# First experts of a fused attention and mixture kernel: weight splits and conversions in other slots, one more product by seven

## The chip, the cores and the metric

One Trainium2 chip, one of its cores. The metric is the device time of one execution in microseconds (us), the median over the runs. PE is TensorE, DVE VectorE, ACT ScalarE, POOL GpSimd, SP the engine that issues nearly all transfers.

## What is computed

```python
kv  = einsum('bhsd,bhse->bhde', k, v)
out = einsum('bhsd,bhde->bhse', q, kv)
x   = out / rms(out) * g_norm              # 2304 tokens x 512
h   = x @ w_in                             # 512 x 2048
x   = (h * sigmoid(h)) @ w_out             # back to 512
p   = domain_probs / sum(domain_probs)     # 4 experts
out = sum_e p[:, e] * (relu(x @ w1[e]) @ w2[e])   # 512 x 1024 each
```

## The kernel before, in words

Tokens stand in three thirds of 768 columns; `acc` in SBUF holds all of them, 512 rows deep. The hidden width is cut into groups of 512: four for the first mixture (the "first experts", groups 0 to 3) and eight for the second. A **step** is one group with one third of the tokens. Steps -12 to -1 are the first experts', 0 to 23 the second's; steps -9 to -7 are group 1, -6 to -4 group 2, -3 to -1 group 3.

A step has a **first product** (tokens by `w1`) and a **second product** (hidden values by `w2`, added to `acc`). The second product of step n runs interleaved with the first product of step n + 1. Every operand is split into a high and a low half: ACT writes the high half (`hi`, L149), DVE or POOL the low half (`lo`, L152), and three matmuls stand for one.

Both products multiply 2 x 2 blocks. "By seven" (`seven_events`, L626) does it with seven block products and sums of blocks (Winograd's form of Strassen); "by blocks" (`plain_events`, L651) with eight. `seven(n)` (L138) says which second products are by seven. Each block product is 12 matmuls of 128x128 by 128x384. For seven, the weights need sums s1 to s4 besides a11, a12, a22 (`SUMS`, L216), the hidden values c11 to c22 need sums t1 to t4 (`sumh`, L451), and the results in PSUM are read after every block product: for the first product by `keep` (ACT, L407) and `add` (DVE, L412), for the second by `gather` (DVE, L457). There is one bank `ps_ox` and one `ps_oz`; a gather must have read its bank before the next block product into it begins, two block products of the second product (four of PE's) after the one it reads. The seven run in the order b11, t1, t2, b22, t3, b21, t4 (`ORDER`, L80), the gathers as `GATHER` (L81) lists them.

The weights of the first experts come as 64-bit integers' words that the kernel turns into floats: `load_wd` (SP), `cv1` and `cv2` (ACT), `cv3` and `cv4` (DVE: L196, L197, L201), `cv5` (POOL, L207). There are two stage buffers, so a load waits for the `cv5` of two conversions before. A group has eight **conversions** of 128x512, four for `w1` and four for `w2`. Then sums (`fsum`, L230) and splits (`fhi`, `flo`, L253 and L258) make the weights of the products; three of a group's seven first weights (numbers 1, 4 and 6) get their low half on POOL.

Nothing schedules at run time. Each event is put at a **slot**, a number; slots count PE's block products, `start[n]` is the first slot of step n, and `after` is the start of the next one. `events` (L707) sorts all events by slot, and each engine takes its own in that order. So a table of slots (`SUM_AT`, `SPLIT_AT`, `CONVERT`, and the numbers in L580 to L587) is the order of every queue. The second experts' weights have tables of their own: `W1_AT` and `W2_AT` (L673 and L677).

```python
put(after + 2 * m, self.again, n, k)          # second product, block m
put(after + 2 * m + 1.1, self.gather, ...)    # L647; 0.25 for m = 6 of the first experts
```

Of the kernel before, what the change touches and what calls it, by code (L numbers as in the profile page):

```python
# [65 lines left out]
class Net:  # L66
# [70 lines left out]

    def seven(self, n):  # L138

        return n >= 1 or n in (-9, -8, -7, -5, -4, -3)  # L140

    def pair(self, n):
        return (n + F1) % NP
# [66 lines left out]
    def quarter(self, e, i, name):  # L210
# [6 lines left out]
        s1=("a21", "a22", ALU.add), s2=("s1", "a11", ALU.subtract), s3=("a11", "a21", ALU.subtract),  # L217
        s4=("a12", "s2", ALU.subtract),
    )

    SUM_AT = {1: (5, 5.1, 6.5, 8), 2: (15.4, 15.5, 16.8, 18), 3: (7.6, 7.7, 12, 14)}
    SPLIT_AT = {
        1: dict(a11=6, s4=7.2, s3=8.6, s1=10.8, s2=11.8, a12=14.8, a22=16),
        2: dict(a11=2.4, a12=4.4, a21=6.4, a22=14.5, s1=15.9, s4=17.1, s3=18.3, s2=29.2),
        3: dict(a11=6, s1=8.5, s2=10.5, s4=12.5, s3=14.5, a12=16, a22=18, a21=18.2),
    }

    CONVERT = {1: (6.5, 9, 18.5, 20.5, 22.5, 25.5, 31, 35), 2: (6, 8.5, 15, 19.2, 20.8, 22.4, 24, 31.8)}
# [317 lines left out]
    def first_events(self, put):  # L546

        pool = self.nc.gpsimd
        for n in range(-F1, 0):
            e, t = self.group(n), self.pair(n)  # L550
            b0, after = self.start[n], self.start[n + 1]
            if e == 0 and t == 2:
                for b, (i, j) in enumerate(self.PLAIN):
                    at, name = b0 + 4 * b, f"c{i + 1}{j + 1}"
# [22 lines left out]
                (self.seven_events if self.seven(n) else self.plain_events)(put, n)  # L577
            if t == 0:
                if e > 0:
                    for name, at in (("s1", -6.6), ("s2", -6.5), ("s3", -1.6), ("s4", -1.5)):  # L580
                        put(b0 + at, self.fsum, e, 0, name)
                    for k in range(7):
                        put(b0 - 9 + 2 * k, self.fhi, e, 0, k)
                        put(b0 - 8.6 + 2 * k, self.flo, e, 0, k, pool if k in (1, 4, 6) else None)
                        if self.A[k][0] == "s":
                            put(b0 + (-1.4 if k == 2 else -8.5 + 2 * k), self.done_sum, e, 0, self.A[k])
                    put(b0 + 3.6, self.done_full, e, 0)  # L587
                    for at, name in zip(self.SUM_AT[e], ("s1", "s2", "s4", "s3")):
                        put(b0 + at, self.fsum, e, 1, name)
                    for name, at in self.SPLIT_AT[e].items():  # L590
                        put(b0 + at, self.fhi, e, 1, name)
                        put(b0 + at + 0.4, self.flo, e, 1, name)
                        if name[0] == "s":
                            put(b0 + max(at + 0.5, self.SUM_AT[e][2] + 0.1 if name in ("s1", "s2") else 0), self.done_sum, e, 1, name)
                    put(b0 + max(*self.SUM_AT[e], *(at for name, at in self.SPLIT_AT[e].items() if name[0] == "a")) + 0.5, self.done_full, e, 1)
                if e + 1 < E1:
                    for i in range(2):
                        for c in range(4):
                            k = 4 * i + c
                            if e == 0 and k < 3:  # L600
                                continue
                            at = b0 + self.CONVERT[e][k] if e else after + 9 + 2.4 * k
                            a = 4 * (e + 1) + c, i
                            if (e, k) != (0, 3):
                                put(max(at - 5.7, b0 + self.CONVERT[e][k - 2] + 1.5) if e and k > 1 else at - 5.7, self.load_wd, *a)
                            put(at, self.cv1, *a)
                            put(at + 0.01, self.cv2, *a)
                            put(at + 0.5, self.cv3, *a)
                            put(at + 0.8, self.cv4, *a)
                            put(at + 1.2, self.cv5, *a)  # L610
            if e == 0 and t == 2:
                for k, name in enumerate(("t1", "t2", "t3", "t4")):
                    at = b0 + 0.5 + 3 * k
# [376 lines left out]
```

## Time and profile before

| what | value |
|---|---|
| median of 3 runs | 1147.36 us (1146.85 to 1147.37) |
| the profiled execution's own time | 1146.34 us |
| its span, first to last instruction | 1144.6 us |
| mean granted TensorE clock | 0.999 |
| PE busy | 1134.5 us (99%), 6673 matmuls |
| DVE busy | 950.2 us (83%) |
| ACT busy | 515.7 us (45%) |
| POOL busy | 335.1 us (29%) |

A row of the timeline gives an instruction's start, its duration, engine, line, what it writes and reads, and in brackets how long its engine had been idle and who released it. A row with x12 is one block product. Matmuls are pipelined, so a product's row is a little longer than the distance to the next. An instruction's duration on DVE and POOL includes time in which it was held up after it had been issued.

### The profile page before, as it was taken

The page shows a single profiled execution, that of the slowest core. Times are in us where ns is not written, and L with a number is a line of the kernel's source. Part 1 is how long each engine was busy: PE and PEld are TensorE (multiplying, and loading weights), DVE is VectorE, ACT ScalarE, POOL GpSimd, SP SyncE. Part 2 cuts the span into 40 slices and gives each one's busy share as a digit, 9 for nine tenths or more (in the row PEclk, how much of TensorE's full clock was granted, in tenths as well). Part 3 has the DMA queues.
Part 4 walks back from the last instruction along what each step waited for, and adds up shares of the span by engine and source line. Part 5 has one row for each costly group of instructions (what it writes and reads, how often), then busy time and mean ns, then how long its engine had stood idle before and what let it go on. Part 6 is the DMA issues. An engine that isn't in the chain of part 4 may idle for free.

```text
span 1144.6 us, 17104 instructions
## 1 busy us (share of the span) xinstructions
PE 1134.5 (99%) x6673; PEld 1128.5 (99%) x6673; DVE 950.2 (83%) x1080; ACT 515.7 (45%) x730; POOL 335.1 (29%) x198
## 2 busy tenths in 40 slices
PE   9999999999999999999999999999999999999998
PEld 8999999999999999999999999999999999999998
DVE  3997768987987587699799899899889889889874
ACT  4885565555554454544333333333333333333334
POOL 4943213331221344132232222232232232223211
PEclk9999999999999999999999999999999999999999
DMA  9967876666656662695675776675686685686604
GB/s 365 361 241 259 296 294 245 219 208 222 229 191 212 196 235 100 249 311 196 237 240 205 234 253 203 217 253 202 216 268 208 204 271 198 205 278 207 207 32 162
DMA packets 70035, 261.23 MB, mean 228 GB/s; under 512 B 7804, under 2 KB 26180, under 8 KB 69444
## 3 DMA queue, kind: packets, MB, share of 16 engines
q1 hardware_dynamic: 69668, 260.11, 65.2%
q8 instruction: 53, 0.87, 0.3%
q14 instruction: 26, 0.21, 0.1%
q10 hardware_dynamic: 288, 0.04, 0.0%
HBM read 222.34 MB, written 37.79 MB: 227 GB/s over the span
## 4 chain that ended last, share of the span: by engine, by line
PE 88%; DVE 6%; DMA 2%; ACT 2%; issue 1%; POOL 0%; SPq 0%; DVEq 0%; ACTq 0%; POOLq 0%
PE ps_x L369 22%; PE ps_ox L369 19%; PE ps_z L369 16%; PE ps_oz L369 15%; PE ps_o L498 9%; PE ps_h L397 4%; DMA kv_raw<-in_kv 2%; DVE hid L152 1%; ACT hid L149 1%; PE p_o L858 1%; PE ps_kv L836 1%; DVE acc L467 1%; DVE f L454 1%; DVE f L414 1%; ACT f L424 1%; DMA wd_raw<-in_wd 1%
## 5 line engine op out<-in xcount | busy, mean ns | idle before, releaser
L149 ACT ACTIVATE hid<-f 128x768 fp32r<-128x768 f32 x231 | 192.1, 843 | 370.4 <-DVE f L454 195.4
L152 POOL TENSOR_TENSOR hid<-f,hid 128x768 fp32r<-128x768 f32 x82 | 162.9, 1987 | 569.9 <-ACT hid L149 438.4
L369 PE MATMUL ps_x<-x,w 128*128 128x384 f32 x1584 | 297.0, 335 | 0.0
L369 PEld LDWEIGHTS ps_x<-x,w 128*128 128x128 f32 x1584 | 277.7, 188 | 0.0
L369 PE MATMUL ps_ox<-hid,w 128*128 128x384 f32 x1392 | 261.4, 335 | 0.6 <-DVE acc L467 0.6
L369 PEld LDWEIGHTS ps_ox<-hid,w 128*128 128x128 f32 x1392 | 243.2, 188 | 1.0 <-ACT hid L149 0.9
L369 PE MATMUL ps_z<-x,w 128*128 128x384 f32 x1188 | 222.8, 335 | 0.0
L369 PEld LDWEIGHTS ps_z<-x,w 128*128 128x128 f32 x1188 | 208.3, 188 | 0.0
L369 PE MATMUL ps_oz<-hid,w 128*128 128x384 f32 x1044 | 196.4, 335 | 1.8 <-DVE acc L467 1.3
L152 DVE TENSOR_TENSOR hid<-f,hid 128x768 fp32r<-128x768 f32 x149 | 153.0, 1028 | 52.3 <-ACT hid L149 52.2
L369 PEld LDWEIGHTS ps_oz<-hid,w 128*128 128x128 f32 x1044 | 182.3, 188 | 3.0 <-DVE acc L467 2.0
L498 PE MATMUL ps_o<-hid,w 128*128 128x384 f32 x672 | 124.2, 334 | 0.0
L454 DVE TENSOR_TENSOR f<-f 128x768 f32<-128x768 f32 x116 | 115.2, 993 | 2.7 <-ACT f L424 1.2
L498 PEld LDWEIGHTS ps_o<-hid,w 128*128 128x128 f32 x672 | 117.3, 188 | 0.0
L467 DVE TENSOR_TENSOR acc<-ps_ox,acc 128x768 f32<-128x768 f32 x109 | 103.6, 951 | 14.1 <-PE ps_ox L369 13.2
L414 DVE TENSOR_TENSOR f<-ps_z,f 128x768 f32<-128x768 f32 x66 | 62.9, 953 | 39.8 <-PE ps_z L369 39.8
L449 DVE SCALAR_TENSOR_TENSOR f<-f,pb 128x768 f32<-128x768 f32 x72 | 86.6, 1203 | 2.5
L467 DVE TENSOR_TENSOR acc<-ps_oz,acc 128x768 f32<-128x768 f32 x85 | 80.8, 951 | 8.9 <-PE ps_oz L369 8.1
L149 ACT ACTIVATE w<-s 128x512 fp32r<-128x512 f32 x88 | 54.9, 624 | 54.9 <-DVE s L292 29.2
L207 POOL TENSOR_TENSOR full<-full,wd_raw 128x512 int32<-128x512 int32 x32 | 47.9, 1497 | 103.8 <-DVE full L201 60.9
L409 ACT ACTIVATE f<-ps_x 128x768 f32<-128x768 f32 x66 | 53.3, 807 | 35.1 <-PE ps_x L369 35.0
L152 DVE TENSOR_TENSOR w<-s,w 128x512 fp32r<-128x512 f32 x74 | 53.3, 727 | 5.4 <-ACT w L149 4.7
(77 smaller groups left out, 955.8 us busy)
## 6 DMA issues: line engine op xcount, KB each, us to landing
x<-x_dram SPq DMA_DIRECT2D x210, 768.0 KB, 4.3
x_dram<-x SPq DMA_DIRECT2D x42, 768.0 KB, 5.2
wd_raw<-in_wd SPq DMA_DIRECT2D x32, 512.0 KB, 4.7
raw<-in_w SPq DMA_DIRECT2D x128, 128.0 KB, 4.6
kv_raw<-in_kv SPq DMA_DIRECT2D x18, 512.0 KB, 10.3
pb<-p_dram SPq DMA_DIRECT2D x24, 384.0 KB, 5.0
q_raw<-in_qt SPq DMA_DIRECT2D x4, 1152.0 KB, 11.6
out<-o SPq DMA_DIRECT2D x6, 512.0 KB, 2.8
```

Source lines behind the costliest of these rows:

```text
L149: self.nc.scalar.activation(t[:, 0], f, AF.Copy)
L152: (eng or self.nc.vector).tensor_tensor(t[:, 1], f, t[:, 0].bitcast(F32), op=ALU.subtract)
L207: self.nc.gpsimd.tensor_tensor(f, f, self.words(c, i, 0, I32), op=ALU.add)
L369: self.nc.tensor.matmul(p[:, f, :HN], w[0][:, a, c : c + 128], x[:, b, kp, :], start=self.FRESH[k] and a == b == kp == 0, stop=b == kp == ...
L397: self.nc.tensor.matmul(p, w[:, u, c : c + 128], self.x[n, f"b{k + 1}{j + 1}"][:, v, kp, :], start=u == v == k == kp == 0, stop=v == k == ...
L409: self.nc.scalar.activation(t, self.of_ps(n, c), AF.Copy)
L414: self.nc.vector.tensor_tensor(t, self.of_ps(n, c), t, op=ALU.add)
L424: self.nc.scalar.activation(self.f[n, name], src, AF.Silu)
L449: self.nc.vector.scalar_tensor_tensor(f, src, 0.0, self.probs(n, int(name[2]) - 1), op0=ALU.max, op1=ALU.mult)
L454: self.nc.vector.tensor_tensor(f, self.f[n, a], self.f[n, b], op=ALU.subtract)
L467: self.nc.vector.tensor_tensor(a, self.of_ps(n, k), a, op=ALU.add)
L498: self.nc.tensor.matmul(self.ps[n, b][:, e, :HN], w[:, u, c : c + 128], h[:, v, kp, :], start=self.count[key] == 1, stop=self.count[key] = ...
```

## The change

Five things in the tables of the first experts. (1) Step -6's second product is by seven instead of by blocks. (2) The first weights of groups 1 to 3 are split at the slots that the second experts use (`SPLIT1_AT`, with `SUM1_AT`) instead of one every two slots from start - 9. (3) Group 2's second weights and their sums stand at the slots of the second experts; a21 is no longer split there. (4) The eight conversions of groups 2 and 3 stand at 13, 16, 18.2, 22.4, 24, 27, 30.4 and 32.4 after the start of the group before. (5) The later slots for the halves of c11, c21 and t4 (`late`), which the second experts had, hold for the first too.

```diff
-        return n >= 1 or n in (-9, -8, -7, -5, -4, -3)
+        return n >= 1 or n in (-9, -8, -7, -6, -5, -4, -3)
...
-    SUM_AT = {1: (5, 5.1, 6.5, 8), 2: (15.4, 15.5, 16.8, 18), 3: (7.6, 7.7, 12, 14)}
+    SUM1_AT = {1: (-7.6, -7.5, -2.6, -2.4), 2: (-7.6, -7.5, -5.1, -4.5), 3: (-7.6, -7.5, -5.1, -4.5)}
+    SPLIT1_AT = {
+        1: (-7.9, -7.8, -6.8, -3.2, 0.5, 6, 6.8),
+        2: (-7.9, -7.8, -6.8, -5.8, 0.5, 6, 6.8),
+        3: (-7.9, -7.8, -6.8, -5.8, 0.5, 6, 6.8),
+    }
+    SUM_AT = {1: (5, 5.1, 6.5, 8), 2: (7.2, 7.5, 9.4, 9.6), 3: (7.6, 7.7, 12, 14)}
     SPLIT_AT = {
         1: dict(a11=6, s4=7.2, s3=8.6, s1=10.8, s2=11.8, a12=14.8, a22=16),
-        2: dict(a11=2.4, a12=4.4, a21=6.4, a22=14.5, s1=15.9, s4=17.1, s3=18.3, s2=29.2),
+        2: dict(a11=6.5, s1=8, s2=8.6, s4=15.5, s3=19.2, a12=20.4, a22=21.5),
...
-    CONVERT = {1: (6.5, 9, 18.5, 20.5, 22.5, 25.5, 31, 35), 2: (6, 8.5, 15, 19.2, 20.8, 22.4, 24, 31.8)}
+    CONVERT = {1: (13, 16, 18.2, 22.4, 24, 27, 30.4, 32.4), 2: (13, 16, 18.2, 22.4, 24, 27, 30.4, 32.4)}
...
-                    for name, at in (("s1", -6.6), ("s2", -6.5), ("s3", -1.6), ("s4", -1.5)):
+                    split = dict(zip(self.A, self.SPLIT1_AT[e]))
+                    sums = dict(zip(("s1", "s2", "s4", "s3"), self.SUM1_AT[e]))
+                    for name, at in sums.items():
                         put(b0 + at, self.fsum, e, 0, name)
-                    for k in range(7):
-                        put(b0 - 9 + 2 * k, self.fhi, e, 0, k)
-                        put(b0 - 8.6 + 2 * k, self.flo, e, 0, k, pool if k in (1, 4, 6) else None)
...
+                    for k, at in enumerate(split.values()):
+                        put(b0 + at, self.fhi, e, 0, k)
+                        put(b0 + at + 0.4, self.flo, e, 0, k, pool if k in (1, 4, 6) else None)
...
-        late = 0 <= n < self.steps - 1
+        late = n < self.steps - 1
         c11, c21, t4 = (5.8, 4.7, 5.6) if late else (4.7, 3.3, 4.6)
```

PE, the end of step -6's second product (`ps_o` are half blocks before, 12 matmuls each in one or more rows; `ps_ox` and `ps_oz` are products by seven; `ps_x` and `ps_z` belong to step -5's first product). Before:

```order
L369 MATMUL ps_z<-x_2589,w_2373 128x384 x12
L498 MATMUL ps_o<-hid,w_2480 128x384 x6
L498 MATMUL ps_o<-hid,w_2622 128x384 x6
L369 MATMUL ps_x<-x_2624,w_2417 128x384 x12
L498 MATMUL ps_o<-hid,w_2480 128x384 x6
L498 MATMUL ps_o<-hid,w_2622 128x384 x6
L369 MATMUL ps_ox<-hid,w_2397 128x384 x12
```

Now:

```order
L375 MATMUL ps_x<-x_2546,w_2352 128x384 x12
L375 MATMUL ps_oz<-hid,w_2748 128x384 x12
L375 MATMUL ps_z<-x_2584,w_2455 128x384 x12
L375 MATMUL ps_ox<-hid,w_2769 128x384 x12
L375 MATMUL ps_x<-x_2623,w_2468 128x384 x12
L375 MATMUL ps_ox<-hid,w_2463 128x384 x12
```

Eight stretches of 12 matmuls into `ps_o` have become seven into `ps_ox` and `ps_oz`; the last row of each is step -5's second product.

DVE in step -7, from the gather of its second block product (the first row) to that of its fourth (the last). L196, L197 and L201 are a conversion, L234 weight sums, L152 low halves (`hid` of hidden values, `w` of weights), L414 `add`, L454 `sumh`, L467 `gather`. Before:

```order
L467 TENSOR_TENSOR acc<-ps_oz,acc 128x2x384
L152 TENSOR_TENSOR hid<-f,hid 128x768
L414 TENSOR_TENSOR f<-ps_z,f 128x768
L454 TENSOR_TENSOR f<-f 128x768
L467 TENSOR_TENSOR acc<-ps_ox,acc 128x2x384
L152 TENSOR_TENSOR hid<-f,hid 128x768
L152 TENSOR_TENSOR w_2181<-full_1647,w_2181 128x512
L196 TENSOR_SCALAR full_1960<-full_1960 128x512
L197 TENSOR_SCALAR full_1960<-full_1960 128x512
L201 SCALAR_TENSOR_TENSOR full_1960<-wd_raw,full_1960 128x512
L467 TENSOR_TENSOR acc<-ps_oz,acc 128x2x384
```

Now (lines behind L207 are six higher):

```order
L473 TENSOR_TENSOR acc<-ps_oz,acc 128x2x384
L196 TENSOR_SCALAR full_1976<-full_1976 128x512
L197 TENSOR_SCALAR full_1976<-full_1976 128x512
L420 TENSOR_TENSOR f<-ps_z,f 128x768
L201 SCALAR_TENSOR_TENSOR full_1976<-wd_raw,full_1976 128x512
L473 TENSOR_TENSOR acc<-ps_ox,acc 128x2x384
L152 TENSOR_TENSOR hid<-f,hid 128x768
L460 TENSOR_TENSOR f<-f 128x768
L152 TENSOR_TENSOR hid<-f,hid 128x768
L240 TENSOR_TENSOR s<-full_1771 128x512
L240 TENSOR_TENSOR s<-s,full_1771 128x512
L152 TENSOR_TENSOR w_2202<-full_1771,w_2202 128x512
```

The fourth gather (L473 on `ps_oz`) is the next row. The two weight sums have come ahead of it, the conversion has moved to an earlier place, and c21's low half to a later one; ahead of this piece two more conversions stand in the step's front now, where one stood.

DVE in step -5, from the gather of its second block product's result to that of the fourth, now (before, the second product in this step was by blocks, with a gather after every second half block):

```order
L473 TENSOR_TENSOR acc<-ps_oz,acc 128x2x384
L420 TENSOR_TENSOR f<-ps_z,f 128x768
L196 TENSOR_SCALAR full_2598<-full_2598 128x512
L197 TENSOR_SCALAR full_2598<-full_2598 128x512
L201 SCALAR_TENSOR_TENSOR full_2598<-wd_raw,full_2598 128x512
L473 TENSOR_TENSOR acc<-ps_ox,acc 128x2x384
L152 TENSOR_TENSOR hid<-f,hid 128x768
L460 TENSOR_TENSOR f<-f 128x768
L152 TENSOR_TENSOR w_2724<-s,w_2724 128x512
L152 TENSOR_TENSOR hid<-f,hid 128x768
L152 TENSOR_TENSOR w_2748<-full_1976,w_2748 128x512
L473 TENSOR_TENSOR acc<-ps_oz,acc 128x2x384
```

A conversion and two low halves of second weights (s3, a12) stand between the two gathers; two conversions and s4 stand ahead of the piece in the same front, which begins with the last gather of step -7's second product.

## Rows read from the trace of the kernel before

**Rows 1.** The page's chain that ended last: shares of the span by engine.

```profile
PE 88%; DVE 6%; DMA 2%; ACT 2%; issue 1%; POOL 0%; SPq 0%; DVEq 0%; ACTq 0%; POOLq 0%
```

**Rows 2.** PE in order of time, steps -7 to -4: start, duration, engine, line, operation.

```profile
219.88 2.25 PE L369 MATMUL ps_oz<-hid,w 128*128 128x384 f32 x12
...
238.66 2.25 PE L369 MATMUL ps_x<-x,w 128*128 128x384 f32 x12
...
251.71 2.40 PE L369 MATMUL ps_oz<-hid,w 128*128 128x384 f32 x12 [0.98 <-DVE acc L467]
...
256.03 2.25 PE L369 MATMUL ps_ox<-hid,w 128*128 128x384 f32 x12
...
293.58 2.25 PE L369 MATMUL ps_x<-x,w 128*128 128x384 f32 x12
...
298.47 2.25 PE L369 MATMUL ps_z<-x,w 128*128 128x384 f32 x12
```

**Rows 3.** DVE in order of time: a gather in step -6, a weight sum in step -5.

```profile
250.70 0.95 DVE L467 TENSOR_TENSOR acc<-ps_oz,acc 128x768 f32<-128x768 f32 x1
...
264.18 0.69 DVE L234 TENSOR_TENSOR s<-full 128x512 f32<-128x512 f32 x1
```

**Rows 4.** DVE in order of time, the front of step -7.

```profile
197.47 0.95 DVE L467 TENSOR_TENSOR acc<-ps_ox,acc 128x768 f32<-128x768 f32 x1
198.46 0.96 DVE L454 TENSOR_TENSOR f<-f 128x768 f32<-128x768 f32 x1
200.34 0.96 DVE L152 TENSOR_TENSOR hid<-f,hid 128x768 fp32r<-128x768 f32 x1 [0.91 <-ACT hid L149]
...
204.82 0.42 DVE L196 TENSOR_SCALAR full<-full 128x512 f32<-128x512 f32 x1
...
206.35 0.95 DVE L467 TENSOR_TENSOR acc<-ps_oz,acc 128x768 f32<-128x768 f32 x1
207.21 1.74 DVE L152 TENSOR_TENSOR hid<-f,hid 128x768 fp32r<-128x768 f32 x1
...
210.87 0.94 DVE L467 TENSOR_TENSOR acc<-ps_ox,acc 128x768 f32<-128x768 f32 x1
211.74 0.94 DVE L152 TENSOR_TENSOR hid<-f,hid 128x768 fp32r<-128x768 f32 x1
212.60 0.68 DVE L152 TENSOR_TENSOR w<-full,w 128x512 fp32r<-128x512 f32 x1
213.44 1.85 DVE L196 TENSOR_SCALAR full<-full 128x512 f32<-128x512 f32 x1
...
216.39 0.95 DVE L467 TENSOR_TENSOR acc<-ps_oz,acc 128x768 f32<-128x768 f32 x1
```

**Rows 5.** POOL in order of time: two undisturbed operations, then the front of step -7.

```profile
154.46 1.30 POOL L207 TENSOR_TENSOR full<-full,wd_raw 128x512 int32<-128x512 int32 x1 [8.84 <-DVE full L201]
...
176.33 1.86 POOL L152 TENSOR_TENSOR hid<-f,hid 128x768 fp32r<-128x768 f32 x1 [14.93 <-ACT hid L149]
...
205.92 2.22 POOL L152 TENSOR_TENSOR hid<-f,hid 128x768 fp32r<-128x768 f32 x1 [7.80 <-issue]
208.10 2.03 POOL L207 TENSOR_TENSOR full<-full,wd_raw 128x512 int32<-128x512 int32 x1
212.91 2.09 POOL L152 TENSOR_TENSOR hid<-f,hid 128x768 fp32r<-128x768 f32 x1 [2.78 <-ACT hid L149]
```

**Rows 6.** DVE and PE in order of time in a step of the second experts.

```profile
577.38 2.33 DVE L152 TENSOR_TENSOR w<-raw,w 128x512 fp32r<-128x512 f32 x1
579.63 0.95 DVE L467 TENSOR_TENSOR acc<-ps_oz,acc 128x768 f32<-128x768 f32 x1
...
582.68 2.25 PE L369 MATMUL ps_oz<-hid,w 128*128 128x384 f32 x12
```

**Rows 7.** The list of waits: engine, line, waited for, us in total, times, longest.

```profile
ACT full L189 <- DMA wd_raw<-in_wd: 12.6, 7, 4.0
```

More of the change, by code (lines that the diff above doesn't have):

```diff
@@ L579, in first_events @@
                 if e > 0:
-                    for name, at in (("s1", -6.6), ("s2", -6.5), ("s3", -1.6), ("s4", -1.5)):
+                    split = dict(zip(self.A, self.SPLIT1_AT[e]))
+                    sums = dict(zip(("s1", "s2", "s4", "s3"), self.SUM1_AT[e]))
+                    for name, at in sums.items():
                         put(b0 + at, self.fsum, e, 0, name)
-                    for k in range(7):
-                        put(b0 - 9 + 2 * k, self.fhi, e, 0, k)
-                        put(b0 - 8.6 + 2 * k, self.flo, e, 0, k, pool if k in (1, 4, 6) else None)
-                        if self.A[k][0] == "s":
-                            put(b0 + (-1.4 if k == 2 else -8.5 + 2 * k), self.done_sum, e, 0, self.A[k])
-                    put(b0 + 3.6, self.done_full, e, 0)
+                        end = max(split[name] + 0.4, *(sums[x] for x, of in self.SUMS.items() if name in of), -99)
+                        put(b0 + end + 0.05, self.done_sum, e, 0, name)
+                    for k, at in enumerate(split.values()):
+                        put(b0 + at, self.fhi, e, 0, k)
+                        put(b0 + at + 0.4, self.flo, e, 0, k, pool if k in (1, 4, 6) else None)
+                    put(b0 + max(*split.values(), *sums.values()) + 0.5, self.done_full, e, 0)
                     for at, name in zip(self.SUM_AT[e], ("s1", "s2", "s4", "s3")):
```

## The prediction

> **What bounds the kernel now.** I read the chain of work that ended last first: 88% of the span lies on PE [rows 1]. So only two things change the time: fewer matmuls, or fewer and more waits of PE. Next, PE in order of time. A product is 12 matmuls. From the product at 219.88 to the one at 238.66 PE starts nine, so each takes (238.66 - 219.88) / 9 = 2.087 us; I call this a slot [rows 2]. From 238.66 to 256.03 PE does seven products in 17.37 us where 14.61 would do: 2.76 us lost. From 293.58 to 298.47 it does two in 4.89 instead of 4.17: 0.72 lost [rows 2]. That is 3.48 us of waiting in the steps that the change touches. The largest piece is the product at 251.71, which waited 0.98 us for DVE's gather at 250.70 [rows 2, 3]: a gather adds a finished product's bank to `acc`, and the next product into that bank may begin about 1.0 us after the gather does.
>
> Third, what makes a gather late. DVE takes its queue in order. Step -7 (197 to 228 us) shows the front half of a step by seven products, from the gather of the step before's last product (197.47) to the fourth gather of this one, which empties `ps_oz` (216.39): 18.92 us [rows 4]. PE needs that gather for the product at 219.88, so it had to begin by 219.88 - 1.01 = 218.87, which is 21.40 after 197.47. Margin: 2.5 us. What fills it:
> - Thirteen long DVE operations (128x768). Starts follow each other 0.87 apart (210.87 and 211.74 [rows 4]), 11.3 in all.
> - Conversions, 1.53 each (204.82 to 206.35) [rows 4].
> - A low half of a weight: 0.61 (its 0.68, less the 0.07 by which neighbours overlap) [rows 4].
> - About 1.1 in which t1's low half waits for ACT: 0.91 idle and the gaps around it (197.47, 198.46, 200.34) [rows 4].
> - The rest is POOL. DVE's 207.21 took 1.74 instead of 0.95 and its 213.44 took 1.85 instead of 0.42, while POOL worked from 205.92, 208.10 and 212.91 [rows 4, 5]. Without POOL the list is 11.3 + 3.06 + 0.61 + 1.1 + 0.2 = 16.3, so POOL made DVE wait 2.6 us. The three POOL operations take 1.86 + 1.30 + 1.86 = 5.0 alone [rows 5]: 0.52 of it.
>
> **The change, part by part.** *Step -6's second product by seven.* PE does 84 matmuls instead of 96: one slot, -2.09 us, all on PE. For it DVE gets 3 more gathers, 4 sums and 1 more low half and loses the low half of a21: 8 x 0.87 - 0.61 = 6.4 us. POOL gets t3's and t4's low halves (3.7), ACT two high halves net. None of this is on PE as long as the gathers stay in time; that is the question below.
>
> *Weight work between the sixth and tenth product.* Ahead of step -6's fourth gather stood the sixth first weight, a11, a12, a21 and a conversion, the weights each waiting for its high half on ACT; the sixth first weight and a11 stay, now just ahead of the gather. That front becomes 11.3 + 1.2 + 1.1 = 13.6, and with two POOL operations (3.7 x 0.52 = 1.9) 15.5 against 21.4. So the waits at 241 to 252 go: -2.76. The 0.72 at step -4's start goes with its cause in part (the plain block's last gather and s2), and I book it as gone, -0.72, and count afresh what comes in its place.
>
> *Conversions spread.* They move out of step -6 and into steps -8, -7, -5 and -4. Step -5 gets five, three in its front; steps -7 and -4 get three in their fronts, where -7 had two and -4 one. With the weight sums moved ahead of the fourth gather too, the fronts are, counted from the last gather as above:
> - Step -5: 11.3 + 3 x 1.53 + 3 x 0.61 (s4, s3, a12) + 1.1 = 18.9.
> - Steps -7 and -4: 11.3 + 4.59 + two sums at 0.69 [rows 3] less overlap, 1.3, + 0.61 + 1.1 = 19.0.
> Each front now holds five POOL operations (three conversions, t3, t4), 3 x 1.30 + 2 x 1.86 = 7.6 alone. How long DVE waits for them no row of before shows, since no front there holds five. Bounds: nothing below 1.6, what one of them cost in a step of the second experts (577.38 took 2.33, where such a low half takes 0.68 at 212.60 [rows 4]) [rows 6]; at most the 7.6. By 0.52 it is 4.0. Laying step -5's queue out by hand, so that a POOL operation runs beside the gathers and adds and stops everything else, I get 0.7 on t2's low half, 1.5 on the third conversion, 0.8 on c21's low half, 1.9 on a12's: 4.9. I take 4.5.
>
> Against the 21.4:
> - Step -5 begins on time: 18.9 + 4.5 = 23.4, PE waits **2.0**.
> - Step -7: 19.0 + 4.5 = 23.5, and DVE enters it late by about 1.0 (step -8: 19 long operations 16.5, five conversions 7.7, two low halves 1.2, 1.1, POOL 10.2 x 0.52 = 5.3, together 31.8 in 29.2, less what the light step -9 lets it do early; ends 0 and 2.6): PE waits **3.1**.
> - Step -4: from the start of step -5's fourth gather DVE still has 8.9 of work (six long operations 5.2, a22's low half 0.6, two conversions 3.1) and 2 x 1.30 x 0.55 = 1.4 of waits for POOL: 23.4 + 8.9 + 1.4 = 33.7, where the next step's gather is ready at 14 slots + 2.0 = 31.2. So step -4 begins 2.5 late: 23.5 + 2.5 = 26.0, PE waits **4.6**, the first of it already for t1 and t2.
> New waits: 9.7. After each of them PE's delay lets DVE catch up, and steps -3 on hold no conversions.
>
> *The rest.* The later high halves of c11, c21 and t4 cost nothing: their products come five slots after or more. The first weights' splits crowd together at the end of the step before their products, each still five slots or more ahead of its product, as in the second experts: zero. A raw weight's load waits in SP's queue for the POOL add two conversions before, and ACT for the load; before, seven such waits cost ACT 12.6 us, 4.0 at most [rows 7]. With DVE late they will come too, but a conversion is now done over ten slots before its weight is split; zero, and 4.0 at most where one stands ahead of t3's high half on ACT.
>
> **The sum.** -2.09 - 3.48 + 9.7 = +4.1 us. The profiled execution took 1146.34, so 1150.4 by it; it lies 1.02 under the median of the runs, 1147.36, so I predict **1151.5**. This kernel's runs tell 0.2% (2.3 us) from no change.
>
> A rule speaks against this change. The row shows a DVE low half that takes 1.74 beside a POOL operation, and a gather that keeps its 0.95 [rows 4]. The Trainium skill, "SBUF — State Buffer", section "Who interferes with whom", says that DVE with two SBUF inputs and a GpSimd operation that reads SBUF shut each other out for the whole instruction, and that a DVE operation with one SBUF input (a gather, whose other input is in PSUM) does not contend. The trace agrees in both. Where only operations of the first kind stood beside POOL, the rule would charge each POOL operation whole: the third rival.
>
> **The rivals.**
> 1. *The margins hold; faster.* In the second experts' steps the same order of weight work runs without a wait: the fourth gather begins at 579.63 and is needed at 582.68 - 1.0 [rows 6], 2.0 us in hand. There DVE also does the four products with the probabilities, which the first experts leave to ACT. If DVE waits for POOL 1.6 to 2.5 in a front, step -5 has no wait, -7 at most 1.1 and -4 at most 2.1. At 2.1 in a front the new waits are about 2: 1147.4 - 5.6 + 2 = 1143.8; with none 1141.8. I put it at **1143.5**. The point from which it decides is 2.5 in a front, where new waits reach 3.3 and the gain 2.3. Against it: 2.6 was waited already with three POOL operations. Chance 0.21.
> 2. *It cancels.* At 2.5 to 3.9 in a front the new waits are 3.3 to 7.9, and the time lies within 2.3 of before, about **1148**. Chance 0.25.
> 3. *POOL stops DVE whole.* 7.6 in a front: step -5 waits 5.1, -7 6.2, -4 8.9; 20.2 in all, **1162**. Against it: the gathers and adds are a third of DVE's work and run beside POOL. Chance 0.05.
> That the seven products are not there can't be: the order shows them.
>
> **How the numbers follow.** The forecast (3.9 to about 6 in a front) has 0.49, and its own range is 1149.7 to 1155. Slower by over 0.2%: 0.49 + 0.05 = 0.54; within: 0.25; faster: 0.21. The range reaches from 1143, which leaves out under half of the first rival, to 1155, which leaves out the third and the forecast's edge.
>
> **What would show it.** Right: 12 fewer matmuls; PE without a wait in step -6; waits of PE for `acc` gathers, the largest in step -4, then -7, then -5, with DVE's operations of 1.5 to 2.6 us beside POOL before each. Wrong: no wait above 1 us from step -8 to -4 (then rival 1), a wait of PE for a weight's or hidden value's half in place of a gather, or waits in step -6 or after -3.

## The result, and the profile after

| | before | after |
|---|---|---|
| median | 1147.11 us (1146.78 to 1147.37, 4 runs) | 1157.54 us (1156.27 to 1157.81, 4 runs) |
| ratio after / before | | 1.0089, 95% interval 1.0071 to 1.0106 |
| the profiled execution | 1146.34, span 1144.6 | 1157.28, span 1155.5 |
| matmuls | 6673 | 6661 |

The change costs 10.4 us. The direction was predicted, the size was not: 4.1 were forecast, and 1157.5 lies above the range (1143 to 1155).

The page of the changed kernel, busy time (part 1) and the chain that ended last, by engine:

```profile
PE 1135.8 (98%) x6661; PEld 1129.6 (98%) x6661; DVE 958.3 (83%) x1087; ACT 516.5 (45%) x732; POOL 339.1 (29%) x200
...
PE 85%; DVE 9%; DMA 3%; ACT 2%; issue 1%; POOL 0%; SPq 0%; DVEq 0%; POOLq 0%; ACTq 0%
```

Twelve matmuls fewer, and still PE is busy 1.3 us longer than before; the share of DVE in the chain grew from 6% to 9% [rows 1]. Where PE waited, and for what, the timeline of PE tells (start, duration, engine, line, operation, in brackets the idle time before and who ended it), steps -7, -5 and -4:

```profile
212.04 2.25 PE L375 MATMUL ps_oz<-hid,w 128*128 128x384 f32 x12
214.51 2.38 PE L375 MATMUL ps_z<-x,w 128*128 128x384 f32 x12 [0.22 <-DVE f L420]
...
218.82 2.25 PE L375 MATMUL ps_x<-x,w 128*128 128x384 f32 x12
224.68 4.21 PE L375 MATMUL ps_oz<-hid,w 128*128 128x384 f32 x12 [3.61 <-DVE acc L473]
228.69 2.81 PE L375 MATMUL ps_z<-x,w 128*128 128x384 f32 x12
231.34 2.25 PE L375 MATMUL ps_ox<-hid,w 128*128 128x384 f32 x12
...
281.42 0.34 PE L375 MATMUL ps_ox<-hid,w 128*128 128x384 f32 x1
283.29 2.21 PE L375 MATMUL ps_ox<-hid,w 128*128 128x384 f32 x11 [1.54 <-DVE w L152]
285.34 2.25 PE L375 MATMUL ps_x<-x,w 128*128 128x384 f32 x12
...
310.43 2.25 PE L375 MATMUL ps_z<-x,w 128*128 128x384 f32 x12
313.05 2.35 PE L375 MATMUL ps_ox<-hid,w 128*128 128x384 f32 x12 [0.36 <-DVE acc L473]
...
322.62 3.66 PE L375 MATMUL ps_oz<-hid,w 128*128 128x384 f32 x12 [5.13 <-DVE acc L473]
326.12 2.25 PE L375 MATMUL ps_z<-x,w 128*128 128x384 f32 x12
```

I call **lost** what the distance between starts exceeds 2.087 us per product [rows 2].
- Step -7, 212.04 to 231.34: six products in 19.30 instead of 12.52, 6.8 lost. 4.3 of it lies ahead of 224.68. The rest is new: the product at 224.68 took 4.01 until the next began, that one 2.65, 2.5 too much, and neither waited for anybody.
- Step -5, 281.42 to 285.34: 1.8 lost, in the middle of a product.
- Step -4, 310.43 to 326.12: 7.3 lost, 5.9 of waits and 1.4 in the slow product behind (322.62 to 326.12 is 3.50).
- Step -6: from 231.34 every distance is 2.09 until step -5. The waits of before at 241 to 252 [rows 2] are gone.

Together 16.0: 12.0 of waits, 3.9 in slow products. With 2.09 for the twelve matmuls and 3.48 for the old waits: 16.0 - 5.6 = +10.4, the measured difference.

The slow products are told by the granted clock. Stretches of the span: length, busy time of PE, PEld, DVE, ACT, POOL, the granted clock, DMA:

```profile
200.00:230.00 30.00, 26.17 (x136) 25.53 (x135) 27.75 (x32) 14.00 (x21) 9.79 (x6) 0.89 0.53 202
230.00:262.00 32.00, 32.00 (x186) 32.00 (x185) 24.48 (x28) 14.99 (x21) 7.48 (x4) 1.00 0.60 206
...
320.00:350.00 30.00, 27.38 (x150) 27.38 (x151) 24.63 (x28) 15.00 (x21) 7.85 (x5) 0.94 0.42 146
```

It was 1.00 everywhere else in these steps and fell only in the stretches in which PE had stood idle 3.61 and 5.13 us: 4.01 against 2.09 is nearly what the lower of its two levels gives (1.2 against 2.4 GHz).

What made the fourth gather late: DVE in the front of step -7, the answer to [rows 4] (its last row is from step -4), and POOL in step -7's front, the answer to [rows 5].

```profile
198.23 0.95 DVE L473 TENSOR_TENSOR acc<-ps_ox,acc 128x768 f32<-128x768 f32 x1
...
205.11 1.49 DVE L152 TENSOR_TENSOR hid<-f,hid 128x768 fp32r<-128x768 f32 x1
...
210.47 1.67 DVE L196 TENSOR_SCALAR full<-full 128x512 f32<-128x512 f32 x1 [0.60 <-ACT full L189]
212.18 1.42 DVE L197 TENSOR_SCALAR full<-full 128x512 int32<-128x512 int32 x1
...
214.98 0.95 DVE L473 TENSOR_TENSOR acc<-ps_ox,acc 128x768 f32<-128x768 f32 x1
216.10 1.22 DVE L152 TENSOR_TENSOR hid<-f,hid 128x768 fp32r<-128x768 f32 x1 [0.18 <-ACT hid L149]
...
219.89 2.20 DVE L240 TENSOR_TENSOR s<-s,full 128x512 f32<-128x512 f32 x1
222.01 1.75 DVE L152 TENSOR_TENSOR w<-full,w 128x512 fp32r<-128x512 f32 x1
223.68 0.94 DVE L473 TENSOR_TENSOR acc<-ps_oz,acc 128x768 f32<-128x768 f32 x1
...
311.14 0.43 DVE L196 TENSOR_SCALAR full<-full 128x512 f32<-128x512 f32 x1 [1.46 <-ACT full L189]
```

```profile
204.46 1.32 POOL L207 TENSOR_TENSOR full<-full,wd_raw 128x512 int32<-128x512 int32 x1 [9.19 <-DVE full L201]
210.01 1.85 POOL L152 TENSOR_TENSOR hid<-f,hid 128x768 fp32r<-128x768 f32 x1 [4.23 <-issue]
211.82 1.49 POOL L207 TENSOR_TENSOR full<-full,wd_raw 128x512 int32<-128x512 int32 x1
215.19 1.32 POOL L207 TENSOR_TENSOR full<-full,wd_raw 128x512 int32<-128x512 int32 x1 [1.89 <-PE ps_oz L375]
219.35 2.19 POOL L152 TENSOR_TENSOR hid<-f,hid 128x768 fp32r<-128x768 f32 x1 [2.85 <-ACT hid L149]
221.50 1.71 POOL L152 TENSOR_TENSOR w<-full,w 128x512 fp32r<-128x512 f32 x1
```

From the last gather of the step before (198.23) to the fourth gather (223.68) are 25.45 us; 21.40 were to be had. Six DVE operations are stretched, by 0.54, 1.25, 0.99, 0.27, 1.51 and 1.07: 5.6 us beside six POOL operations of 9.9 us together. The sixth, which I had not counted, is the low half of the first weight a12 at 221.50. The gather at 214.98 keeps its 0.95 while POOL works from 215.19; the operation after it (216.10) ends 0.81 after POOL does (216.10 + 1.22 against 215.19 + 1.32), about its own length: it reads as run once POOL was done. The Trainium skill, "SBUF — State Buffer", section "Who interferes with whom", says that DVE and GpSimd shut each other out of a shared pair of ports, and that a DVE operation with one input from SBUF does not need it, except in DVE's 2-port modes, which tensor_scalar can enter. The gather agrees with the rule. The TENSOR_SCALAR at 210.47 and 212.18 have one input from SBUF too and were held by 1.25 and 0.99, so for them the exception counts, which the prediction's sentence on this rule leaves out.

Step -4 has the same shape: its front runs from 296.07 to 321.62, 25.55 us, with 5.1 of stretches and the 1.46 of idle time at 311.14. That is no late load. ACT forms the conversion's first words in its queue behind a Silu, the Silu waits for DVE's addition at 308.74, and the conversion next in DVE's queue waits for ACT: a circle through DVE's own queue.

### The profile page after: what moved, and what is told of

The parts are those of the page before. It is cut to its first block, busy times and chain, and to the rows that moved or that the text cites. A ratio compares the mean times of both kernels' runs of the same rounds, so it can differ in the third digit from the quotient of the medians.

```text
span 1155.5 us, 17101 instructions
## 1 busy us (share of the span) xinstructions
PE 1135.8 (98%) x6661; PEld 1129.6 (98%) x6661; DVE 958.3 (83%) x1087; ACT 516.5 (45%) x732; POOL 339.1 (29%) x200
## 4 chain that ended last, share of the span: by engine, by line
PE 85%; DVE 9%; DMA 3%; ACT 2%; issue 1%; POOL 0%; SPq 0%; DVEq 0%; POOLq 0%; ACTq 0%
PE ps_x L375 21%; PE ps_ox L375 19%; PE ps_z L375 16%; PE ps_oz L375 14%; PE ps_o L504 9%; PE ps_h L403 4%; DMA kv_raw<-in_kv 2%; DVE hid L152 2%; DVE acc L473 1%; DVE f L460 1%; DVE full L201 1%; DVE full L196 1%; DVE w L152 1%; DVE f L420 1%; PE p_o L866 1%
## 5 line engine op out<-in xcount | busy, mean ns | idle before, releaser
L149 ACT ACTIVATE hid<-f 128x768 fp32r<-128x768 f32 x234 | 194.6, 843 | 384.2 <-DVE f L460 208.8
L152 POOL TENSOR_TENSOR hid<-f,hid 128x768 fp32r<-128x768 f32 x84 | 165.4, 1969 | 549.5 <-ACT hid L149 414.0
L375 PE MATMUL ps_ox<-hid,w 128*128 128x384 f32 x1440 | 270.7, 335 | 1.9 <-DVE w L152 1.5
L375 PEld LDWEIGHTS ps_ox<-hid,w 128*128 128x128 f32 x1440 | 251.5, 188 | 2.7 <-DVE w L152 1.9
L375 PE MATMUL ps_oz<-hid,w 128*128 128x384 f32 x1080 | 206.2, 339 | 8.7 <-DVE acc L473 8.7
L375 PEld LDWEIGHTS ps_oz<-hid,w 128*128 128x128 f32 x1080 | 191.5, 190 | 9.8 <-DVE acc L473 9.4
L152 DVE TENSOR_TENSOR hid<-f,hid 128x768 fp32r<-128x768 f32 x150 | 152.7, 1019 | 52.2 <-ACT hid L149 52.0
L473 DVE TENSOR_TENSOR acc<-ps_ox,acc 128x768 f32<-128x768 f32 x113 | 107.4, 950 | 16.8 <-PE ps_ox L375 16.1
L504 PE MATMUL ps_o<-hid,w 128*128 128x384 f32 x576 | 106.2, 334 | 0.0
L504 PEld LDWEIGHTS ps_o<-hid,w 128*128 128x128 f32 x576 | 100.5, 188 | 0.0
L473 DVE TENSOR_TENSOR acc<-ps_oz,acc 128x768 f32<-128x768 f32 x88 | 83.6, 950 | 10.0 <-PE ps_oz L375 9.3
L207 POOL TENSOR_TENSOR full<-full,wd_raw 128x512 int32<-128x512 int32 x32 | 48.4, 1513 | 116.3 <-DVE full L201 71.4
L149 ACT ACTIVATE w<-s 128x512 fp32r<-128x512 f32 x88 | 54.9, 623 | 47.1 <-DVE s L298 30.5
L152 DVE TENSOR_TENSOR w<-s,w 128x512 fp32r<-128x512 f32 x74 | 52.2, 713 | 6.6 <-ACT w L149 5.9
## 6 DMA issues: line engine op xcount, KB each, us to landing
q_raw<-in_qt SPq DMA_DIRECT2D x4, 1152.0 KB, 11.4
```

The lines of the kernel that those rows point to most:

```text
L149: self.nc.scalar.activation(t[:, 0], f, AF.Copy)
L152: (eng or self.nc.vector).tensor_tensor(t[:, 1], f, t[:, 0].bitcast(F32), op=ALU.subtract)
L207: self.nc.gpsimd.tensor_tensor(f, f, self.words(c, i, 0, I32), op=ALU.add)
L375: self.nc.tensor.matmul(p[:, f, :HN], w[0][:, a, c : c + 128], x[:, b, kp, :], start=self.FRESH[k] and a == b == kp == 0, stop=b == kp == ...
L473: self.nc.vector.tensor_tensor(a, self.of_ps(n, k), a, op=ALU.add)
L504: self.nc.tensor.matmul(self.ps[n, b][:, e, :HN], w[:, u, c : c + 128], h[:, v, kp, :], start=self.count[key] == 1, stop=self.count[key] = ...
```

## The experiments

The **theory**: the conversions and the weight work stand in fronts that have no room for them, POOL lengthens them, and the clock falls behind the long waits. **Rivals**: the moved weight sums alone do it; DVE's work alone, without POOL; the seven products of step -6. "Floor" is the median of before that was taken beside the run, less 5.57 (2.09 + 3.48); "lost" is read from each kernel's timeline of PE, the slow products included.

| run | what | us | before | lost in step -7 | -5 | -4 | elsewhere |
|---|---|---|---|---|---|---|---|
| after | the change | 1157.54 | 1147.11 | 6.8 | 1.8 | 7.3 | 0 |
| e1 | group 2's conversions earlier | 1151.32 | 1146.70 | 0.4 | 1.9 | 7.7 | 0 |
| e2 | group 3's conversions in second halves | 1155.96 | 1146.70 | 6.8 | 0.9 | 4.6 | 3.2 |
| e3 | both | 1150.41 | 1146.70 | 0.4 | 1.0 | 4.7 | 3.1 |
| e4 | no POOL adds | 1148.41 | 1146.70 | 1.9 | 0 | 4.8 | 0 |
| e5 | first weights behind the gather | 1154.18 | 1146.84 | 4.7 | 1.8 | 6.4 | 0 |
| e8 | e5, ACT's order mended | 1154.00 | 1146.73 | 4.8 | 1.8 | 6.3 | 0 |
| e6 | e5 with other conversions | 1150.00 | 1146.84 | 0.3 | 4.6 | 1.3 | 2.5 |
| e9 | e8, step -5 eased | 1152.98 | 1146.73 | 4.7 | 0.8 | 7.1 | 0 |
| e7 | PE kept busy in the waits | 1153.91 | 1146.84 | 4.4 | 1.8 | 6.0 | 0 |
| e10 | step -6 by four blocks | 1152.03 | 1147.18 | 5.9 | 0 | 2.6 | 0 |
| e11 | best with seven | 1145.69 | 1147.18 | 0.3 | 0.9 | 0.4 | 2.3 |
| e12 | best with four blocks | 1143.78 | 1147.20 | 0.3 | 0 | 0 | 0 |

Floor and losses give each time within 0.9 us (e10 and e12 with 3.48 alone as the floor), so the losses name all of it.

### e1, e2, e3: other places for the conversions

```diff
-    CONVERT = {1: (13, 16, 18.2, 22.4, 24, 27, 30.4, 32.4), 2: (13, 16, 18.2, 22.4, 24, 27, 30.4, 32.4)}
+    CONVERT = {1: (9, 11, 13, 15.5, 19, 22.4, 24.2, 26.6), 2: (13, 16, 18.2, 22.4, 24, 27, 30.4, 32.4)}
```
e2 leaves entry 1 and takes `2: (11.4, 17.4, 22.4, 24.4, 30.5, 36.2, 38.4, 44.5)`; e3 has both entries.

Expected of e1:

> The second group's conversions are done before step -7's front (in steps -9 and -8 alone); everything else as in the changed kernel, the third group's conversions too. Theory (queue: three conversions and their POOL adds, ahead of the fourth gather beside the moved weight sums, make that gather late, and PE's clock falls after the long wait): step -7's loss of 6.8 us goes (4.3 of waits, 2.5 of products at the lower clock), at most 1 us of it comes back in step -8; the time is 1157.5 - 6.8 = 1150.7, 1150 to 1152, and steps -5 and -4 lose what they did. Rival B (the moved weight sums or the seventh-product form of step -6 make the waits, the conversions don't): step -7 keeps its wait of about 3.6 us for the fourth gather, the time stays at 1156.5 to 1158.

Measured: 1151.32 (ratio to before 1.0043, 1.0027 to 1.0058). Step -7's 6.8 have fallen to 0.4, as the theory had it, and the sums still stand where they stood: the sums alone make no wait there.

Expected of e2:

> The third group's conversions stand mostly in the second halves of the steps -6 to -3, behind the fourth gather; the second group's as in the changed kernel. Theory (queue): steps -5 and -4 lose their 1.9 and 7.3 us no more, step -7 keeps its 6.8: 1157.5 - 9.2 = 1148.3, 1147.5 to 1150. Rival B (the moved sums make the waits): step -4 keeps its wait of 5.1 us, and the time stays at 1156.5 to 1158. Between them (about 1152): the conversions make the lateness with which step -4 begins, the sums the rest.

Measured: 1155.96. Neither: step -4 keeps 4.6 although one conversion is left in its front, and the late conversions cost 3.2 in the steps after. In e3's trace, DVE ahead of step -4's fourth gather:

```profile
307.34 0.68 DVE L240 TENSOR_TENSOR s<-full 128x512 f32<-128x512 f32 x1
308.06 2.22 DVE L240 TENSOR_TENSOR s<-s,full 128x512 f32<-128x512 f32 x1
310.20 1.75 DVE L152 TENSOR_TENSOR w<-full,w 128x512 fp32r<-128x512 f32 x1
311.88 0.95 DVE L473 TENSOR_TENSOR acc<-ps_oz,acc 128x768 f32<-128x768 f32 x1
```

4.5 us of weight work, 2.6 of them stretches by POOL: there the sums have their part.

Expected of e3:

> Both tables: no conversion of the second and third group ahead of a fourth gather that has no room. Theory (queue): the changed kernel's three gains stay (2.09 for twelve matmuls, 3.48 for the old waits) and its 16.0 us of new loss go: 1147.1 - 5.6 = 1141.5, 1141 to 1144. Rival B: 1156 to 1158. A third way: the moved conversions now make DVE late in the second halves, and PE waits there for ps_ox gathers; 1144 to 1148.

Measured: 1150.41 (1.0033, 1.0020 to 1.0045). The two edits add up (5.8 and 1.2 us under the changed kernel, each less its own before, and 6.7 together), but 9.2 us of loss stay. A third of it (3.1) is the third way foreseen, and 4.7 are step -4's.

### e4: without POOL's additions

```diff
-                            put(at + 1.2, self.cv5, *a)
+                            put(at + 1.2, self.cv5 if e == 0 else self.no_cv5, *a)
```

The kernel then leaves out the low words of these weights.

> Left out: the POOL add of the low words in the conversions of the groups after the first (all DVE and ACT work stays, at the changed kernel's places). Theory (DVE waits for POOL): a front loses three of its six POOL operations, its waits for POOL fall from about 5.5 to about 2.6 (what three cost in the kernel before); step -7 then waits 1.0, step -4 about 2, step -5 none, and the clock stays up: 1147.1 - 5.6 + 3 = 1144.6, 1143 to 1147. Rival C (the DVE work itself is too long, POOL costs nothing): 1156.5 to 1158. Rival D (POOL holds DVE for each operation's whole length): three adds take 3.9 us out of each front, and only step -4 waits, under 0.5: 1142.

Measured: 1148.41 (1.0012, 1.0003 to 1.0021), 8.7 us less than the changed kernel, each less its own before, and above the theory's 1143 to 1147. POOL's additions take no DVE time of their own, and without them more than half of the 16.0 is gone: rival C is out. So is rival D, as step -4 still waited 3.05 where under 0.5 was expected:

```profile
222.62 2.35 PE L378 MATMUL ps_oz<-hid,w 128*128 128x384 f32 x12 [1.67 <-DVE acc L476]
...
313.58 3.87 PE L378 MATMUL ps_oz<-hid,w 128*128 128x384 f32 x12 [3.05 <-DVE acc L476]
```

Behind 1.67 the product took its 2.19, behind 3.05 it took 3.67 (to 317.25). The theory's price was too low: the three POOL operations left in step -7's front (198.04 to 221.62) held DVE for 3.9 us, not for the 2.6 of before (the DVE operations at 209.61, 217.79 and 219.93 took 1.68, 2.22 and 1.77 instead of 0.42, 0.69 and 0.68).

### e7: PE kept busy

```diff
+        for _ in range({(-8, 1): 16, (-5, 1): 22}.get((n, k), 0)):
+            nc = self.nc.tensor
+            nc.matmul(self.ps[n + 1, "x"][:, 1, 384:512], self.ident, self.ident, start=True, stop=True)
```

> The changed kernel with matmuls that nothing reads (128 columns, into a bank's columns that nothing uses) ahead of the two products that wait longest: 16 in step -7, 22 in step -4. The waits themselves stay. Theory (PE's clock fell to its lower level because PE had stood idle 3.6 and 5.1 us): the granted clock stays at 1.00 in these steps, the products behind the waits take 2.09 us again, and 1.9 + 0.6 + 1.4 = 3.9 us come back: 1153.6, 1153 to 1155. Rival (these products are slow for another cause, their operands or late weights): they keep 3.5 to 4.0 us, and the time stays at 1157 to 1158, or rises by what the added matmuls overrun.

Measured: 1153.91 (1.0060, 1.0047 to 1.0074). The added matmuls write into a bank in which sums are being formed, so e7 is there to time the waits and is no kernel to use. A window over step -7 (columns as above; the changed kernel's clock was 0.89 there), and PE in step -7:

```profile
200.00:230.00 30.00, 29.76 (x181) 29.25 (x180) 28.02 (x32) 13.47 (x20) 9.80 (x6) 1.00 0.54 210
...
221.46 3.73 PE L524 MATMUL ps_x<-ident 128*128 128x128 f32 x32
225.25 2.36 PE L375 MATMUL ps_oz<-hid,w 128*128 128x384 f32 x12
227.44 2.25 PE L375 MATMUL ps_z<-x,w 128*128 128x384 f32 x12
229.53 2.25 PE L375 MATMUL ps_ox<-hid,w 128*128 128x384 f32 x12
```

The product waits as long as before and then takes 2.19 instead of 4.01, the next 2.09 instead of 2.65. 3.4 us came back (10.43 over before became 7.07) where 3.9 were expected. So the slow products are the clock's, and the clock fell because PE stood idle. The Trainium skill, "TensorE: Matmul & The Clock Gate", section "Part 1: The HAM clock gate", says that the throttled clock is the default state and that activity of PE releases it. This run agrees: with matmuls that nothing reads the granted clock stayed at 1.00.

### e5 and e8: the first weights behind the fourth gather

```diff
-    SUM1_AT = {1: (-7.6, -7.5, -2.6, -2.4), 2: (-7.6, -7.5, -5.1, -4.5), 3: (-7.6, -7.5, -5.1, -4.5)}
+    SUM1_AT = {1: (-7.6, -7.5, -2.6, -2.4), 2: (-6.75, -6.65, -5.1, -4.5), 3: (-6.75, -6.65, -5.1, -4.5)}
...
-        2: (-7.9, -7.8, -6.8, -5.8, 0.5, 6, 6.8),
+        2: (-7.2, -7.1, -6.2, -5.8, 0.5, 6, 6.8),
```
Entry 3 of SPLIT1_AT as entry 2; e8 has -5.8 and -5.6 in place of -6.2 and -5.8.

> The conversions stand as in the changed kernel; the low half of the first weight a11, the sums s1 and s2 (DVE) and a12's low half (POOL) of the steps -6 and -3 are put just behind the fourth gather instead of just ahead of it. Theory (the front is too long, whatever is taken out of it): the fronts of steps -7 and -4 lose 4.4 to 4.5 us (0.61 + 2.1 + 1.7 in the changed kernel's trace, the last two of them stretched by POOL); step -7 comes to 21.0 against the 21.4 it has and waits no more, step -4 to about 1.5 with no clock loss, step -5 keeps 1.9: 1157.5 - 6.8 - 5.8 = 1144.9, 1143.5 to 1147. Rival (the work only moves and is late in the second half, for the ps_ox gathers or the first weights): 1148 to 1152. Rival (only conversions matter, since step -7's loss went with them alone): step -7 keeps its wait, 1156 to 1158.

Measured: 1154.18. The fourth gather came at 218.90, 20.95 us after the front's beginning and in time, but PE waited 2.44 one product later, for ACT's copy of c22. That copy stood in ACT's queue behind s2's high half:

```profile
223.93 0.63 ACT L149 ACTIVATE w<-s 128x512 fp32r<-128x512 f32 x1 [3.90 <-DVE s L240]
224.47 0.79 ACT L415 ACTIVATE f<-ps_z 128x768 f32<-128x768 f32 x1
```

Expected of e8, which puts the copy first:

> As e5, but with the high halves of s2 and s1 behind c22's copy in ACT's queue (0.4 and 0.2 slots later), so that ACT no longer stands before that copy until DVE has formed s2. Everything of the conversions as in the changed kernel. Theory: e5's front was on time (20.95 us in step -7), its loss came from ACT waiting 3.9 us for s2 with c22's copy behind; with that gone only step -5's 1.9 for s3 and about 1.3 in step -4 are left: 1141.5 + 3.2 + 0.5 (step -7's start) = 1145.2, 1144 to 1147. Rival (the weight work in the second half costs in any order): PE waits for ps_z or ps_ox products there, 1149 to 1154.

Measured: 1154.00. The copy now starts at 219.85, and the wait is another product on, for the fifth gather. DVE in step -7 of e8:

```profile
218.81 0.95 DVE L473 TENSOR_TENSOR acc<-ps_oz,acc 128x768 f32<-128x768 f32 x1
219.67 1.70 DVE L152 TENSOR_TENSOR w<-full,w 128x512 fp32r<-128x512 f32 x1
221.30 1.77 DVE L240 TENSOR_TENSOR s<-full 128x512 f32<-128x512 f32 x1
...
226.31 0.95 DVE L473 TENSOR_TENSOR acc<-ps_ox,acc 128x768 f32<-128x768 f32 x1
```

The rival of both runs was right in kind (e5's time lies above its 1148 to 1152, e8's at the edge of 1149 to 1154), and my picture of a front with one deadline too small. Every gather is a deadline. DVE's arrears are carried from one to the next until a stretch without weight work takes them up; an operation moved behind one gather stands ahead of the next.

### e6 and e9: two attempts at step -5

e6 is e5 with e1's entry 1, entry 2 at `(8.5, 10.5, 13.5, 17, 22.4, 24.2, 27.2, 30)` and s3's split at 17.5; e9 is e8 with `2: (11, 15, 18.2, 22.4, ...)` and s3 at 17.9.

> Both: sums and first weights behind the fourth gather as in e5, the second group's conversions ahead of step -7 as in e1, the third group's at one or two in each half step, and s3's split 1.7 slots earlier. Theory: no front is over 21.4 us and s3 is in time: nothing is lost but the twelve matmuls' gain stays: 1141.5, at most 1144. Rival (weight work in the second half makes that late): 1145 to 1149.

> As e8, and for step -5: the third group's first two conversions 2 and 1 slots earlier (into step -6's second half, where DVE stood idle for PE) and s3's split 1.3 slots earlier. Theory: step -5 loses nothing (its front has one conversion fewer and s3's low half is done before the third conversion), step -4 enters earlier: 1142 to 1144.5, faster than before. Rival: step -6 or -5 now waits in its second half (as it did in e6 with three conversions there): 1145 to 1149.

Measured: 1150.00 and 1152.98. e6 fell to its rival (its time lies 1.0 above that one's range): three conversions in step -6's second half make that half late (2.5 lost), and step -5 after it loses 4.6. e9 did what neither text has: step -5 loses 0.8 instead of 1.8, as hoped, but step -4 loses 7.1 instead of 6.3, and step -7 keeps e8's loss, 4.7, which e9's edit does not touch and its expectation took for gone.

### e10: step -6 by four blocks again

```diff
-        return n >= 1 or n in (-9, -8, -7, -6, -5, -4, -3)
+        return n >= 1 or n in (-9, -8, -7, -5, -4, -3)
...
-    SUM_AT = {1: (5, 5.1, 6.5, 8), 2: (7.2, 7.5, 9.4, 9.6), 3: (7.6, 7.7, 12, 14)}
+    SUM_AT = {1: (5, 5.1, 6.5, 8), 2: (15.4, 15.5, 16.8, 18), 3: (7.6, 7.7, 12, 14)}
...
-        2: dict(a11=6.5, s1=8, s2=8.6, s4=15.5, s3=19.2, a12=20.4, a22=21.5),
+        2: dict(a11=2.4, a12=4.4, a21=6.4, a22=14.5, s1=15.9, s4=17.1, s3=18.3, s2=29.2),
```

> The changed kernel with one part undone: step -6's second product by four blocks again, with the second weights' table of before; conversions and first weights as changed. Theory (conversions and first weights fill the fronts; the seven products of step -6 only add to the lateness with which step -4 begins): step -7 keeps its 6.8, step -5 has no wait for s3, step -4 keeps 4.2 of its waits and 1.4 of clock; with the twelve matmuls back the time is 1157.5 + 2.1 - 1.9 - 1.7 = 1156.0, up to 1157.5 where step -6 waits again. Rival (DVE's extra 6.4 us and POOL's 3.7 for the seven products make the loss of steps -5 and -4): both steps' 9.2 go, 1157.5 + 2.1 - 9.2 = 1150.4.

Measured: 1152.03 (1.0042, 1.0028 to 1.0056): between the two, nearer the rival. Step -7 keeps 5.9, step -5 loses nothing, and step -4 loses 2.6 where it lost 7.3:

```profile
318.56 2.38 PE L375 MATMUL ps_oz<-hid,w 128*128 128x384 f32 x12 [2.29 <-DVE acc L473]
320.78 2.25 PE L375 MATMUL ps_z<-x,w 128*128 128x384 f32 x12
```

So with the conversions where the change puts them, the seven products, together with the places of group 2's second weights that e10 undoes with them (parts 1 and 3 of the change), save 2.1 us on PE and cost steps -5 and -4 1.8 + 4.7 = 6.5. I had expected 3.6 of that; the lateness they hand to step -4 is larger than I took it, and the clock goes with it (no loss behind 2.29 here, 1.4 behind 5.13).

### e11 and e12: the best versions

e11 (seven products): e1's entry 1, `2: (11, 15, 18.2, 22.4, 24.5, 28, 37.6, 41.2)`, s3 at 17.9, e8's places for entry 3 of the first weights. e12 (four blocks): e10 with e1's entry 1 and `2: (13, 16, 18.2, 22.4, 24, 27, 30.4, 38)`.

> An attempt at less DVE work before each gather of the steps -5 and -4: the second group's conversions as in e1, the third group's at 11 to 28 slots with the last two in step -4's second half, s3 earlier as in e9, the first weights of step -3 behind the fourth gather as in e8. Theory (lateness adds up over a whole step, each gather is a deadline): step -7 loses nothing, step -5 under 1, step -4 0 to 2: 1143 to 1145. Rival (the steps -6 to -4 have too little DVE time in all, and the waits only move, as in e6, e8 and e9): 1148 to 1152.

> As e10 (step -6's second product by four blocks, first weights as changed), with the second group's conversions ahead of step -7 as in e1 and the third group's last one 5.6 slots later, out of step -4's front. Theory: step -7 loses nothing as in e1, step -4's front is 2.4 us shorter, which is about what it still lost in e10 (2.6): 1152.0 - 5.9 - 2.4 = 1143.7, 1143 to 1145.5; that the seven products of step -6 are not worth their 2.1 us would then show by a time under e11's 1145.7. Rival (the waits only move on, to the fifth gather of step -4 and to step -3, as with the late conversions in e2, e3 and e11): 1146 to 1148.

Measured: e11 1145.69 (0.9987, 0.9978 to 0.9996), just off its upper edge; 2.3 are still lost behind step -4's front, most of it at two waits for `acc` gathers (339.86 and 357.66) that come after the places where the last two conversions now stand; what makes these gathers late was not followed up. e12 **1143.78** (0.9970, 0.9959 to 0.9981), the figure expected, faster than both kernels. Its windows over the front of step -7, and steps -5 and -4 (columns as above):

```profile
200.00:230.00 30.00, 29.94 (x173) 29.60 (x172) 27.70 (x30) 13.97 (x19) 6.79 (x4) 1.00 0.58 197
262.00:294.00 32.00, 32.00 (x186) 32.00 (x185) 26.18 (x38) 17.70 (x27) 7.18 (x5) 1.00 0.74 279
294.00:326.00 32.00, 32.00 (x186) 32.00 (x185) 28.80 (x36) 16.41 (x23) 9.94 (x6) 1.00 0.62 206
```

PE is full and its clock at the upper level. All that e12 wins on before is the 3.48 of old waits. The twelve matmuls did not pay in any version tried; e12's own tables with the seven products were not run, and whether a table exists with which they pay (the floor is 1141.6) is left open. No run undoes part (5), the later slots; e12 has them and loses 0.3, so by themselves they are no cause.

## Why the prediction was right and wrong

- **Twelve matmuls, -2.09**: right, 6661.
- **The old waits, -3.48**: right. No wait in step -6, and e12 stands 3.4 under before by them alone.
- **Step -5, 2.0**: 1.8, but the wait in the trace is another: the product of the weight s3 waited for s3's low half (283.29), two products ahead of the one that the fourth gather holds up; the half stood in DVE's queue behind all three conversions. My own list had a wait for a weight's half as a sign against the reasoning, and for this step it is one. Still, the wait for s3 only hides the one forecast. DVE in the changed kernel, the front's first gather, s3's low half and the fourth gather:

```profile
263.54 0.95 DVE L473 TENSOR_TENSOR acc<-ps_ox,acc 128x768 f32<-128x768 f32 x1
...
282.55 0.69 DVE L152 TENSOR_TENSOR w<-s,w 128x512 fp32r<-128x512 f32 x1
...
286.30 0.95 DVE L473 TENSOR_TENSOR acc<-ps_oz,acc 128x768 f32<-128x768 f32 x1
```

  The front took 22.8 (18.9 of work as reckoned, 3.9 for POOL where 4.5 stood), and DVE entered it 0.4 late. The bank was free at about 287.3; without the wait for s3 its product was due at 285.6, two products behind 281.42. So about 1.7 would have been waited there in any case. That is worked out from these rows; no run shows it by itself.
- **Step -7, 3.1**: waits 4.3. DVE entered the front 0.2 late, not 1.0 (four products from 212.04 the waiting one was due at 220.4; less 1.0 and 21.40 that is 198.0, and DVE entered at 198.23). The work was 19.0 as reckoned (25.45 less 5.6 and 0.8). The term that failed is **the waits for POOL, taken as 4.5**: 5.6, since I counted five POOL operations and there are six; the first weight a12's low half moved into the front with its sums. The five cost 4.6 (the first five stretches), the sixth 1.07. That 4.5 was right for five is partly luck, for the rate is no constant: of what the POOL operations take alone (7.6 for the five, 5.0 for three) it was 0.52 before, 0.60 here, 0.51 in step -5 and 0.78 in e4. To the 5.6 come 0.8 us of DVE waiting for ACT (0.60 and 0.18), which "the rest" booked at zero.
- **Step -4, 4.6**: waits 5.9. Entered 1.8 late, not 2.5; in the front 5.1 for POOL and 1.46 of idle for ACT. The rule for the later lateness was right in kind, the front again too short.
- **The clock, booked at nothing**: 3.9. This is the largest failed term: with it the forecast would have been 1155.4. The waits of before, up to 0.98 us [rows 2], had shown no slow product behind them, and I carried that over to waits of 3 to 5 us which I forecast myself. What the runs showed in its place: the granted clock fell behind the two long waits, and e7, which keeps PE busy in them, gets 3.4 back.
- **Lateness by the seven products**: I gave them 6.4 us of DVE and called none of it on PE as long as the gathers stay in time. They did not, and e10 prices the part, with the second weights' places, at 6.5 of loss.
- **The rivals**: the margins held in none of the steps -7, -5 and -4 of the change as it was; with the conversions elsewhere they did (e1 for step -7, e12 for all). POOL stopping DVE whole is refuted by the 4.6 that the five cost where it has 7.6.
- **Two sums**: the terms of the fronts come to 18.8 (step -5) and 18.9 (steps -7 and -4), not to 18.9 and 19.0; nothing hangs on it.

Of the 6.3 us between forecast and result, 3.9 are the clock and 2.3 the waits (12.0 against 9.7).

## What to carry to other kernels

Where one engine empties banks for another, add up its arrears from gather to gather over the whole step, each gather a deadline: moving work behind one of them only moved the wait (e5, e8), and what helped was to take it to a step that is light (e1, e12). A PE saving that gives the bound engine's helper more to do is priced by that helper's slack, not by the matmuls saved (e10). And a wait of PE that one forecasts at several microseconds needs a second term for the slow products behind it.

## What was not expected of the hardware

The clock's loss does not grow evenly with the wait. Products behind waits of 3.61 and 5.13 us cost 2.5 and 1.4 too much; behind 2.80 (e3) 1.7 and behind 2.47 (e8) 1.7; behind 2.02 us of e6, which followed several shorter waits, again 1.7; behind 2.29 (e10) and 1.67 (e4) nothing. The granted clock says the same: it was 0.79 from 312 to 320 us of e3 and from 276 to 284 us of e6, 0.86 from 222 to 234 us of e8, and 1.00 from 300 to 330 us of e10 and from 200 to 230 us of e4. So in these runs the length of a wait alone did not tell whether the clock fell. The price where it fell was 1.4 to 2.5 us each time.
